# Eight operand turns on TensorE instead of by DMA, and a new order table, in a clustered-attention and MoE kernel

## The chip, the cores and the metric

The kernel runs on one core of a Trainium2 chip. The metric is the device time of one execution in microseconds (us). Beside it stand the span and the rows of one profiled execution. Five engines take part, each with its own queue of instructions: TensorE (PE in the rows; PEld is its loading of weights), VectorE (DVE), ScalarE (ACT), GpSimd (POOL) and SyncE (SP), which here issues all DMAs.

## The reference

```python
mask = q_assign[:, :, :, None] == k_assign[:, :, None, :]      # argmax over 16 centroids, per head
scores = np.where(mask, scale * np.matmul(q, k.transpose(0, 1, 3, 2)), -1000000000.0)
attn = softmax(scores)
x = (attn @ v).transpose(0, 2, 1, 3).reshape(3072, 512)
h = x @ w_in                                                   # 512 -> 2048
P = a[0] + a[1] * h + a[2] * h**2 + a[3] * h**3
Q = 1.0 + abs(b[0]) * abs(h) + abs(b[1]) * h**2
out = (P / (Q + 1e-06)) @ w_out                                # 2048 -> 512
```

(The softmax is abridged.) There are 4 batches, 8 heads, 768 tokens and 64 columns a head; a query attends only to keys of its own cluster.

## The kernel before, in words

All work is written down first as a list of operations (`Plan.op`), each with its engine, its tiles and the tiles it claims. `ORDER` then gives for every engine the sequence in which these operations are issued, as a list of their numbers; this table was found ahead of time by a search with a planner's durations, and while the kernel is built the table alone decides. SBUF tiles come from rings of buffers (`buf`), PSUM tiles from rings of banks (`bank`): tag "s" has two slots, for scores and products.

Heads are worked on in pairs, four pairs to a batch (so `sk_1` below is head pair 1 of the batch in hand). `prep` (from line 916 on) loads q and k of a pair, finds a power-of-two scale for each (squares on ScalarE, a maximum over the partitions by a transpose at line 964, a 1x1 maximum `m1` at 966 and a matmul at 968 that spreads it), and splits each into a high and a low f16 half, in tiles `tk` and `tq` of [128, 2, 6, 128], tokens on the partitions. There are four such tiles a pair: k1, q1, k2, q2. Each must be turned, so that the 128 columns lie on the partitions: `turn` (line 1059) does it with one DMA transpose of twelve 128x128 blocks, `sk` from `tk` and `sq` from `tq`. From the turned k1 and q1 come the logits against the centroids (`ptl`, line 1085), from those the one-hot cluster rows (line 1116) that are written into k2 and q2, and only then are k2 and q2 turned.

Batch 0 goes through `attend_keys`: scores `s` (1301), their row maxima `top` on VectorE (1310), the maxima written as correction rows into `tq` (to line 1344), a second turn of q2, the product `z` (1362) with keys on the partitions, its exponential on ScalarE, the context `px` (1381, 1387), and normalising (1409 to 1440, 1424 on TensorE). Batches 1 to 3 go through `attend` (scores at 1181, masked maximum at 1197, exponential, turn of the probabilities by DMA at 1241, context at 1254). `moe` has the first product `ph` (1511), the rational function on VectorE, ScalarE and GpSimd, and the second product `po` (1622). The weights of the MoE are loaded (`rwi`, `rwo`), scaled and converted (`wwi`, `wwo`, lines 669 to 757) while batch 0 is under way. `v_scale` loads v of a batch once ahead of its use (`rvm`, four loads a batch), squares it on ScalarE (line 526 is the helper that issues every ScalarE activation) and finds its scale (783 to 790). `centroid_norm` (566 to 602) prepares the centroids (`cslot`).

Of the kernel before, what the change touches and what calls it, by code (L numbers as in the profile page):

```python
# [10 lines left out]
F32 = mybir.dt.float32  # L11
F32R = mybir.dt.float32r
F16 = mybir.dt.float16
# [6 lines left out]
P = 128  # L20
# [7 lines left out]
K = {'ghd': 0.0, 'rvp': 0, 'look': 62.89, 'mulp': 0.4, 'sub': 0, 'xn': 14, 'NR': 8, 'sgp': 1, 'scp': 1, 'vsc': 0.75, 'sup0': 0, 'stk': 2, 'lop': 0, 'mgp': 0, 'rvn': 2, 'tq2': 2, 'at': 3, 'es': 4, 'vn': 3, 'ah': 5, 'rel': 0, 'twin': 1}  # L28
# [36 lines left out]
""",  # L65
    "DVE": """
# [313 lines left out]
def clustered_attention_moe_kernel(  # L380
# [89 lines left out]
    def token(name, cap):  # L470
        return Buf(None, name, cap, False)
# [1271 lines left out]
```

## Time and profile before

| what | value |
|---|---|
| three runs | 928.95, 930.76 (median), 934.13 us |
| the profiled execution | 927.86 us |
| its span | 926.1 us |
| busy in the span | PE 93%, DVE 87%, ACT 82%, POOL 65% |
| first row maximum of batch 0 (`top`) | 37.73 us from the span's start |
| first MoE product (`ph`) | 209.43 us |

A busy share is an average over the whole span. The two last lines mark borders within it: before 209.43 the program works on batch 0's attention and on the weights (called stage A), afterwards the MoE of one batch runs beside the attention of the next. In rows, x is the number of instructions that were put together, and a bracket tells how long the engine sat idle before and what ended that.

### The profile page before, as it was taken

Reading aid. Unit: us, or ns where it says so; the run is one execution under the profiler, and the core shown is the slowest. Engines: PE = TensorE matmul, PEld = TensorE weight load, DVE = VectorE, ACT = ScalarE, POOL = GpSimd, SP = SyncE. Lnnn points to the kernel's source line nnn. Section 1 sums busy time; section 2 is a strip of 40 time slices with the busy share of each in tenths; the row PEclk is TensorE's granted clock in tenths of the full one; section 3 lists DMA queues with packets and bytes.
Section 4 is the critical chain, followed back from the end, with each engine's and each line's share of the span. In section 5 each row is a group of like instructions: output and inputs, shape, how many; then the busy total and the mean of one; then the engine's idle time right before and its main releaser. Section 6 shows DMA issues by size and latency. Waiting matters only on the chain. (4 is left out here: it accounts for less than half of the span.)

```text
span 926.1 us, 20282 instructions
## 1 busy us (share of the span) xinstructions
PE 859.2 (93%) x7705; PEld 586.4 (63%) x7705; DVE 809.5 (87%) x1618; ACT 763.8 (82%) x1182; POOL 604.0 (65%) x627
## 2 busy tenths in 40 slices
PE   1559998997999999999999999999999999999997
PEld 1346675765676666667667676666666667766664
DVE  5789899658999999999999999999999998777776
ACT  5656675878998999998999999999998898766674
POOL 1347627398888776888888788868877766322221
PEclk9979999999999999999999999999999999999999
DMA  9996774666677797886869698898758667500000
GB/s 280 295 259 186 171 172 125 184 135 148 124 131 166 138 202 145 165 168 156 157 110 201 123 168 167 173 145 169 161 107 163 123 140 107 83 24 24 1 24 23
DMA packets 357345, 132.95 MB, mean 144 GB/s; under 512 B 335104, under 2 KB 351488, under 8 KB 357248
## 3 DMA queue, kind: packets, MB, share of 16 engines
q1 hardware_dynamic: 357248, 131.67, 67.5%
q8 instruction: 60, 0.98, 0.4%
q14 instruction: 37, 0.30, 0.1%
HBM read 41.98 MB, written 6.29 MB: 52 GB/s over the span
## 5 line engine op out<-in xcount | busy, mean ns | idle before, releaser
L1622 PE MATMUL po<-wout,u 128*128 128x512 f16 x1152 | 266.1, 379 | 1.4 <-ACT ob L526 0.8
L1511 PE MATMUL ph<-x,win 128*128 128x256 f16 x2304 | 266.1, 273 | 1.2 <-DVE x L1270 0.9
L1511 PEld LDWEIGHTS <-win 128*128 128x128 f16 x2304 | 225.1, 98 | 39.7 <-issue 3.2
L1551 POOL TENSOR_TENSOR s<-s,u 128x512 f32<-128x512 f32 x96 | 131.0, 1382 | 117.9 <-ACT s L526 85.7
L1622 PEld LDWEIGHTS <-u 128*128 128x128 f16 x1152 | 111.0, 98 | 122.2 <-issue 3.4
L1234 DVE SCALAR_TENSOR_TENSOR ah<-s,su,ah 128x768 f16<-128x768 f32 x144 | 143.3, 1012 | 8.9 <-ACT ah L526 7.5
L1197 DVE TENSOR_SCALAR_CACHE_REDUCE s<-s,cc 128x768 f32<-128x768 f32 x144 | 144.6, 1018 | 7.4 <-PE s L1181 6.8
L526 ACT ACTIVATE ah<-s,su 128x768 f16<-128x768 f32 x144 | 127.1, 904 | 15.3 <-ACT s L526 7.2
L526 ACT ACTIVATE s<-s,nm 128x768 f32<-128x768 f32 x144 | 126.5, 879 | 12.8 <-DVE s L1197 9.6
L1574 POOL TENSOR_TENSOR s<-s,u 128x512 f32<-128x512 f32 x72 | 103.5, 1448 | 28.7 <-ACT u L526 28.5
L1181 PE MATMUL s<-sk,sq 128*128 128x384 f16 x576 | 113.6, 328 | 8.5 <-DVE ah L1234 3.9
L1611 POOL TENSOR_TENSOR u<-s,u 128x512 f16<-128x512 f32 x72 | 86.5, 1213 | 30.6 <-ACT u L526 16.9
L1181 PEld LDWEIGHTS <-sq 128*128 128x128 f16 x576 | 52.7, 98 | 52.3 <-DVE ah L1234 13.0
L1254 PE MATMUL px<-at,vhi 128*64 128x256 f16 x864 | 74.8, 275 | 1.2 <-DVE df L1100 0.7
L526 ACT ACTIVATE u<-ph 128x512 f32<-128x512 f32 x96 | 57.5, 601 | 19.9 <-PE ph L1511 19.4
L1532 DVE TENSOR_TENSOR t<-ph,t 128x512 f32<-128x512 f32 x96 | 65.4, 682 | 9.0 <-ACT t L526 8.7
L1254 PE MATMUL px<-at,vlo 128*64 128x256 f16 x432 | 61.3, 273 | 0.0
L1604 DVE SCALAR_TENSOR_TENSOR s<-s,t 128x1024 f32<-128x1024 f32 (+1 forms) x49 | 58.7, 1197 | 1.7 <-POOL s L1574 0.7
L1254 PEld LDWEIGHTS <-vhi 128*64 128x64 f16 x864 | 47.9, 110 | 15.7 <-issue 8.2
L526 ACT ACTIVATE u<-t 128x1024 f16<-128x1024 f32 (+1 forms) x49 | 51.2, 1045 | 6.1 <-DVE t L1594 3.0
L526 ACT ACTIVATE t<-ph,gk 128x512 f32<-128x512 f32 x72 | 56.1, 784 | 0.0
L1537 DVE SCALAR_TENSOR_TENSOR t<-t,gk,ph 128x512 f32<-128x512 f32 x72 | 53.0, 740 | 0.9
(213 smaller groups left out, 1520.7 us busy)
## 6 DMA issues: line engine op xcount, KB each, us to landing
rwi<-in_moe_w_in_dram SPq DMA_DIRECT2D x16, 512.0 KB, 5.4
rwo<-in_moe_w_out_dram SPq DMA_DIRECT2D x16, 512.0 KB, 5.4
rk<-in_k_dram SPq DMA_DIRECT2D x32, 192.0 KB, 3.3
rq<-in_q_dram SPq DMA_DIRECT2D x32, 192.0 KB, 3.0
rvm<-in_v_dram SPq DMA_DIRECT2D x16, 384.0 KB, 5.6
rv<-in_v_dram SPq DMA_DIRECT2D x16, 384.0 KB, 4.0
out_dram<-ob SPq DMA_DIRECT2D x11, 512.0 KB, 3.2
at<-ah SPq DMA_TRANSPOSE x144, 3.9
```

What stands on the lines that cost most here:

```text
L526: lambda: nc.scalar.activation(out=out(), in_=in_(), func=func, **{a: (x() if callable(x) else x) for a, x in kw.items()}),
L1181: nc.tensor.matmul(sc.ap[:, i, :SH], lhsT=st["q" + x].ap[:, j, t, :], rhs=st["k" + x].ap[:, j, ks, :].rearrange("p t c -> p (t c)"), start ...
L1197: lambda nm=nm, view=view: ts(out=view(), in0=view(), scalar1=cc.ap, scalar2=None, op0=ALU.mult, op1=ALU.min, accum_out=nm.ap),
L1234: lambda part=part, view=view, su=su: stt(out=part(1), in0=view(), scalar=su.ap, in1=part(0), op0=ALU.mult, op1=ALU.subtract),
L1254: nc.tensor.matmul(px.ap[j * D : (j + 1) * D, :], lhsT=vv.ap[:, j, kt, :], rhs=at[j].ap[:, p_, kt].rearrange("p t c -> p (t c)"), start=(i ...
L1511: nc.tensor.matmul(ph[i].ap[:, fi * TW : (fi + 1) * TW], lhsT=win[f // 4][:, wpart, c, f % 4 * P : (f % 4 + 1) * P], rhs=xs[c].ap[:, xpart ...
L1532: lambda i=i, th=th, ph=ph: tt(out=th[i].ap, in0=ph[i].ap, in1=th[i].ap, op=ALU.mult),
L1551: lambda i=i, sh=sh, uh=uh: nc.gpsimd.tensor_tensor(out=sh[i].ap, in0=sh[i].ap, in1=uh[i].ap, op=ALU.mult),
L1574: lambda i=i, sh=sh, uh=uh: nc.gpsimd.tensor_tensor(out=sh[i].ap, in0=sh[i].ap, in1=uh[i].ap, op=ALU.mult),
L1604: lambda tw=tw, sw=sw: stt(out=sw(), in0=sw(), scalar=2.0, in1=tw(), op0=ALU.subtract, op1=ALU.mult),
L1611: lambda i=i, sh=sh, gl=gl, g16=g16, e=(nc.vector if gld else nc.gpsimd): e.tensor_tensor(out=gl[i].ap, in0=sh[i].ap, in1=g16()[:, 0, i * ...
L1622: nc.tensor.matmul(po[ti].ap, lhsT=g16()[:, part, c0 : c0 + P], rhs=wout[f // 4][:, wpart, f % 4], start=(k == 0 and f == f_first), stop=( ...
```

## The change

`turn` gets a second way. For head pairs 0 and 1 of batch 0 (`'pet': '_01'`) each of the four tiles is turned by twelve TensorE transposes into a PSUM bank of tag "s", and one copy of 1536 columns brings it to SBUF: on ScalarE for k, on VectorE for q. That is eight turns out of 68 of `sk` and `sq`; the second turn of q2, behind the correction rows, stays a DMA. The 1x1 maxima now lie in one of four zeroed [128, 1] columns, and the spreading matmul uses all 128 rows of `ones`. The `ORDER` table is replaced as a whole. `avs` and `xl` have values with which nothing differs.

```diff
@@ K
-... 'rel': 0, 'twin': 1}
+... 'rel': 0, 'twin': 1, 'pet': '_01', 'avs': 3}
@@ set-up
+    columns = [cp.tile([P, 1], F32, name=f"column{i}") for i in range(4)]
+    def column(name):
+        return Buf(lambda i: (name, columns[i])[1], "m1", len(columns), False)
...
+    ident16 = cp.tile([P, P], F16, name="ident16")
+    nc.gpsimd.tensor_copy(out=ident16, in_=ident)
...
+    for x in columns:
+        nc.vector.memset(x, 0.0)
@@ v_scale, and the same in prep
-        m1 = buf([1, 1], F32, "m1", f"vmm{b}", 4)
-        dve(195, lambda: nc.vector.tensor_reduce(out=m1.ap, in_=pt.ap[0:1, :], axis=AX.X, op=ALU.max), [pt], [m1], vt)
+        m1 = column(f"vmm{b}")
+        dve(195, lambda: nc.vector.tensor_reduce(out=m1.ap[0:1], in_=pt.ap[0:1, :], axis=AX.X, op=ALU.max), [pt], [m1], vt)
...
-            "PE", 310, lambda: nc.tensor.matmul(pb.ap, lhsT=ones[0:1, :], rhs=m1.ap, start=True, stop=True),
-            [m1], [pb], vt, mode=2,
+            "PE", 310, lambda: nc.tensor.matmul(pb.ap, lhsT=ones, rhs=m1.ap, start=True, stop=True),
+            [m1], [pb], vt,
@@ prep
-        def turn(x, u):
+        def turn(x, u, by_pe=False):
+            if by_pe:
+                tb_ = bank([P, 2 * NT, P], F16, "s", f"pt{x}{n}", 2)
+                def blocks(x=x, tb_=tb_):
+                    for i in range(2 * NT):
+                        nc.tensor.transpose(
+                            out=tb_.ap[:, i], in_=tm[x].ap.rearrange("p h t c -> p (h t) c")[:, i], identity=ident16
+                        )
...
+                op("PE", 1000, blocks, [tm[x]], [tb_], u, [st[x]])
+                if x[0] == "k":
+                    act(ac(2 * NT * P, 0, True), copied, source, AF.Copy, [tb_], [st[x]], u)
+                else:
+                    dve(dc(2 * NT * P), lambda: nc.vector.tensor_copy(out=copied(), in_=source()), [tb_], [st[x]], u)
+                return
...
+        by_pe = b == 0 and str(hp) in kn("pet", "")
         for x in ("k1", "q1"):
-            turn(x, vt + kc("p2", b, 2))
+            turn(x, vt + kc("p2", b, 2), by_pe)
...
         for x in ("k2", "q2"):
-            turn(x, vt + kc("p4", b, 4))
+            turn(x, vt + kc("p4", b, 4), by_pe)
```

What the new table does shows at three places. In its rows a name carries the pair (with `rvm`, `rwi` and `rwo` the piece) and a running number, and line numbers of the changed kernel are some 9 to 35 higher. The first place is SyncE's queue near its start. Before, behind the loads of the first k and q (`rk_0`, `rq_0`), it holds these loads and turns:

```order
L540 DMA rvm_2_123<-in_v_dram 128x2x384
L540 DMA cslot<-in_centroids_dram 128x64
L540 DMA rvm_1_127<-in_v_dram 128x2x384
L540 DMA rvm_0_129<-in_v_dram 128x2x384
L540 DMA rvm_0_131<-in_v_dram 128x2x384
L540 DMA rwi_2_136<-in_moe_w_in_dram 128x1024
L540 DMA rwi_1_138<-in_moe_w_in_dram 128x1024
L540 DMA rvm_3_145<-in_v_dram 128x2x384
L540 DMA rwi_0_171<-in_moe_w_in_dram 128x1024
L1059 DMA_TRANSPOSE sk_0_182<-tk_0_133 128x12x128
L540 DMA rk_1_189<-in_k_dram 128x384
L1059 DMA_TRANSPOSE sq_0_206<-tq_0_142 128x12x128
```

After the change it begins with:

```order
L549 DMA cslot<-in_centroids_dram 128x64
L549 DMA rk_0_129<-in_k_dram 128x384 x2
L549 DMA rq_0_132<-in_q_dram 128x384 x2
L549 DMA ab<-in_moe_b_dram 128x2
L549 DMA rwi_2_137<-in_moe_w_in_dram 128x1024
L549 DMA rvm_3_141<-in_v_dram 128x2x384
L549 DMA ab<-in_moe_a_dram 128x4
L549 DMA rwi_1_160<-in_moe_w_in_dram 128x1024
L549 DMA rvm_0_162<-in_v_dram 128x2x384
L549 DMA rwi_0_166<-in_moe_w_in_dram 128x1024
L549 DMA rk_1_217<-in_k_dram 128x384 x2
L549 DMA rvm_1_224<-in_v_dram 128x2x384
```

The centroids come first instead of behind five loads, a pair's turns are gone from it, and of the 16 `rvm` loads only the four of batch 0 stand here; those of batch 1 are issued shortly ahead of the first `ph`, the other eight behind it.

The second place is VectorE's queue just ahead of the first row maximum of pair 0. Before:

```order
L674 SCALAR_TENSOR_TENSOR wwo_0_335<-rwo_1_304,wwo_0_335 128x512
L618 TENSOR_SCALAR ev_408<-vp_ln 128x1
L621 RECIPROCAL ev_408<-ev_408 128x1
L787 TENSOR_REDUCE vmm_411<-vt_399 1x1
L681 SCALAR_TENSOR_TENSOR wwo_0_335<-rwo_1_304,wwo_0_335 128x512
L1036 SCALAR_TENSOR_TENSOR tq_1_318<-rq_1_235,qsc_1_373,tq_1_318 128x12x64
L618 TENSOR_SCALAR wie<-wip_ln 128x1
L621 RECIPROCAL wis<-wie 128x1
L1052 COPY tk_1_428<-tk_1_296 128x12x64
L1052 COPY tq_1_430<-tq_1_318 128x12x64
L1310 TENSOR_REDUCE top_0_439<-s_0_0_1_419 128x1
```

After the change (`ptq` is the PSUM bank with the turned q blocks):

```order
L1085 COPY sq_0_411<-ptq_0_393 128x1536
L678 TENSOR_SCALAR wwo_0_334<-wwo_0_334 128x512
L1019 RECIPROCAL qsc_1_385<-qsc_1_385 128x1
L683 SCALAR_TENSOR_TENSOR wwo_0_334<-rwo_1_337,wwo_0_334 128x512
L690 SCALAR_TENSOR_TENSOR wwo_0_334<-rwo_0_246,wwo_0_334 128x512
L1061 COPY tk_1_458<-tk_1_257 128x12x64
L1045 SCALAR_TENSOR_TENSOR tq_1_344<-rq_1_255,qsc_1_385,tq_1_344 128x12x64
L709 SCALAR_TENSOR_TENSOR wig_435,wia_465<-wig_435,ident 128x128
L690 SCALAR_TENSOR_TENSOR wwo_0_334<-rwo_1_337,wwo_0_334 128x512
L1061 COPY tq_1_484<-tq_1_344 128x12x64
L678 TENSOR_SCALAR wwo_1_463<-wwo_1_463 128x512
L1342 TENSOR_REDUCE top_0_492<-s_0_4_1_467 128x1
```

The second copy of pair 0 now stands in front of the maxima, among the same kind of weight conversions and the split of pair 1.

The third place is TensorE's queue around the first `ph`. Before, it ends stage A with the scores of batch 1 and the last normalising product of batch 0:

```order
L1181 LDWEIGHTS sq_0_2627
L1181 MATMUL s_0_0_1_2744<-sk_0_2617,sq_0_2627 128x384
L968 MATMUL kb_2_2752<-km_2_2736,ones 128x1
L1424 MATMUL px_3_2_2661<-rs_3_2_2727,pick 128x128 x2
L1511 LDWEIGHTS win_103
L1511 MATMUL ph_0_0_0_2770<-x_0_0_1321,win_103 128x256
```

After the change, `ph` follows a product z of pair 3, third block of queries:

```order
L1394 MATMUL z_3_2_1_0_2670<-sq_3_1502,sk_3_1212 128x256
L1394 LDWEIGHTS sk_3_1763
L1394 MATMUL z_3_2_1_0_2670<-sq_3_1830,sk_3_1763 128x256
L1546 LDWEIGHTS win_113
L1546 MATMUL ph_0_0_0_2683<-x_0_0_1150,win_113 128x256
```

And some forty rows behind it stand what came ahead of `ph` before:

```order
L1212 LDWEIGHTS sq_0_2557
L1212 MATMUL s_0_0_0_2725<-sk_0_2581,sq_0_2557 128x384
L1456 MATMUL px_3_1_2610<-rs_3_1_2677,pick 128x128 x2
L1212 LDWEIGHTS sq_0_2308
L1212 MATMUL s_0_0_1_2737<-sk_0_2221,sq_0_2308 128x384
```

So scores of batch 1 and the last context and normalising products of batch 0 have moved behind the first `ph`.

## Rows read from the trace of the kernel before

**Rows 1.** The page: busy times, and TensorE in forty slices of the span.

```profile
PE 859.2 (93%) x7705; PEld 586.4 (63%) x7705; DVE 809.5 (87%) x1618; ACT 763.8 (82%) x1182; POOL 604.0 (65%) x627
...
PE   1559998997999999999999999999999999999997
```

**Rows 2.** Busy times of the engines in four stretches; the first line names the columns.

```profile
core 0: us, PE busy (x) PEld busy (x) DVE busy (x) ACT busy (x) POOL busy (x), PEclk, DMA share, GB/s
0.00:36.10 36.10, 9.55 (x85) 6.96 (x85) 22.24 (x77) 21.53 (x45) 8.60 (x25) 1.00 0.99 297
36.10:74.80 38.70, 27.16 (x189) 17.20 (x189) 33.16 (x74) 21.75 (x40) 16.73 (x20) 0.82 1.02 274
74.80:157.20 82.40, 76.28 (x890) 53.05 (x890) 75.72 (x151) 53.65 (x92) 49.98 (x72) 1.00 0.64 158
...
240.00:800.00 560.00, 553.04 (x4803) 374.61 (x4801) 525.62 (x1066) 520.35 (x801) 440.71 (x407) 1.00 0.79 150
```

**Rows 3.** The same view for four other stretches: up to the first maximum, then the rest.

```profile
0.00:37.70 37.70, 11.15 (x90) 7.79 (x91) 23.80 (x81) 21.53 (x45) 8.60 (x25) 1.00 0.98 297
37.70:169.20 131.50, 113.25 (x1215) 78.03 (x1215) 117.35 (x241) 81.95 (x142) 68.19 (x92) 0.95 0.74 192
37.70:74.80 37.10, 25.55 (x184) 16.37 (x182) 31.59 (x69) 21.75 (x40) 16.73 (x20) 0.82 1.03 274
175.30:209.40 34.10, 31.59 (x455) 23.85 (x455) 16.83 (x53) 27.93 (x49) 29.21 (x48) 1.00 0.57 128
```

**Rows 4.** VectorE in order of time: start, duration, operation, idle time before and releaser.

```profile
8.57 0.23 DVE L566 TENSOR_TENSOR cslot<-cslot 128x64 f32<-128x64 f32 x1 [7.20 <-DMA cslot<-in_centroids_dram]
...
9.77 0.16 DVE L978 TENSOR_SCALAR qsc<-qb 128x1 int32<-128x1 int32 x1 [0.35 <-PE qb L968]
...
12.32 1.02 DVE L1036 SCALAR_TENSOR_TENSOR tk<-rk,ksc,tk 128x768 f16<-128x768 f32 x1 [0.58 <-DMA rwi<-in_moe_w_in_dram]
...
13.25 0.35 DVE L1052 COPY tk<-tk 128x768 f16<-128x768 f16 x1
...
169.00 0.19 DVE L1344 TENSOR_SCALAR tq<-rest 128x12 f16<-128x12 f32 x1
```

**Rows 5.** TensorE in order of time, from pair 3's z to the first `ph`.

```profile
175.30 1.36 PE L1362 MATMUL z<-sq,sk 128*128 128x256 f16 x11 [0.20 <-DMA sq<-tq]
...
200.24 2.81 PE L1381 MATMUL px<-at,rv 128*64 128x256 f32 x24
202.98 1.52 PE L1387 MATMUL px<-at,ones 128*32 128x128 f32 x48
...
209.43 1.47 PE L1511 MATMUL ph<-x,win 128*128 128x256 f16 x12
```

**Rows 6.** TensorE in order of time: a single transpose and two groups of sixteen products.

```profile
5.15 0.37 PE L964 MATMUL kt<-ident,sumk 128*1 128x128 f32 x1 [5.15 <-ACT tk L526]
...
30.33 1.89 PE L695 MATMUL wig<-wwi 128*128 128x128 bf16 x16
...
70.84 1.09 PE L695 MATMUL wig<-wwi 128*128 128x128 bf16 x16
```

**Rows 7.** Groups by line and form: busy us, mean ns of one | idle before, releaser.

```profile
L1310 DVE TENSOR_REDUCE top<-s 128x1 f32<-128x768 f32 x48 | 43.5, 947 | 1.2 <-PE s L1301 1.1
...
L526 ACT ACTIVATE at<-z,cc 128x768 f32<-128x768 f32 x48 | 41.8, 896 | 5.9 <-PE z L1362 5.9
...
L526 ACT ACTIVATE ob<-po,g 128x1024 f32<-128x1024 f32 x8 | 8.9, 1113 | 0.1
...
L526 ACT ACTIVATE rvm<-rvm 128x768 f32<-128x768 f32 x16 | 13.3, 834 | 8.1 <-DMA rvm<-in_v_dram 4.9 <-POOL tk L1116 3.2
```

**Rows 8.** DMA issues: the centroids, with their size and us from issue to landing.

```profile
cslot<-in_centroids_dram SPq DMA_DIRECT2D x1, 32.0 KB, 5.5
```

**Rows 9.** Line 1059, the turns by DMA, in the first 81 us.

```profile
DMA to landing us min/median/max: 4.2/5.0/7.9
```

**Rows 10.** ScalarE in order of time: one conversion that waited for its load.

```profile
40.15 0.67 ACT L526 ACTIVATE wwi<-rwi 128x512 f32<-128x512 f32 x1 [4.20 <-DMA rwi<-in_moe_w_in_dram]
```

More of the change, by code (lines that the diff above doesn't have):

```diff
@@ L25 @@
 M_BIG, M_MID, M_LOW = 2.0 ** 15, 2.0 ** 7, 2.0 ** -4
-K = {'ghd': 0.0, 'rvp': 0, 'look': 62.89, 'mulp': 0.4, 'sub': 0, 'xn': 14, 'NR': 8, 'sgp': 1, 'scp': 1, 'vsc': 0.75, 'sup0': 0, 'stk': 2, 'lop': 0, 'mgp': 0, 'rvn': 2, 'tq2': 2, 'at': 3, 'es': 4, 'vn': 3, 'ah': 5, 'rel': 0, 'twin': 1}
+K = {'ghd': 0.0, 'rvp': 0, 'look': 62.89, 'mulp': 0.4, 'sub': 0, 'xn': 14, 'NR': 8, 'sgp': 1, 'scp': 1, 'vsc': 0.75, 'sup0': 0, 'stk': 2, 'lop': 0, 'mgp': 0, 'rvn': 2, 'tq2': 2, 'at': 3, 'es': 4, 'vn': 3, 'ah': 5, 'rel': 0, 'twin': 1, 'pet': '_01', 'avs': 3}
 ORDER = {
     "ACT": """
[32 rows of a table removed]
[32 rows of a table added]
 """,
     "DVE": """
[45 rows of a table removed]
[45 rows of a table added]
 """,
     "PE": """
[26 rows of a table removed]
[26 rows of a table added]
 """,
     "POOL": """
[20 rows of a table removed]
[20 rows of a table added]
 """,
     "SP": """
[12 rows of a table removed]
[12 rows of a table added]
 """,
@@ L206 @@
     MORE = {("ACT", "POOL"): 95.0, ("DVE", "POOL"): 60.0, ("POOL", "ACT"): -30.0, ("ACT", "ACT"): 120.0, ("PE", "DVE"): 65.0, ("DVE", "ACT"): 50.0}
-    DMA = {"turn": (1440.0, 4100.0, 1700.0), "w": (430.0, 3900.0, 1350.0), "v": (450.0, 3900.0, 1100.0),
-           "qk": (430.0, 3000.0, 500.0), "few": (350.0, 2500.0, 200.0), "o2": (340.0, 3800.0, 1310.0), "o1": (340.0, 2300.0, 700.0)}
-    QUEUE = 950.0
+    DMA = {"turn": (1500.0, 4100.0, 1750.0), "w": (500.0, 4000.0, 1400.0), "v": (500.0, 4000.0, 1150.0),
+           "qk": (500.0, 3100.0, 520.0), "few": (350.0, 2500.0, 200.0), "o2": (340.0, 3800.0, 1310.0), "o1": (340.0, 2300.0, 700.0)}
+    QUEUE = 1300.0
     SWITCH = 105.0
@@ L455, in share @@
         return math.floor((i + 1) * f + 1e-6) > math.floor(i * f + 1e-6)
-    KEYMAJOR = {(0, int(hp)) for hp in kn("km", "0123")}
+    KEYMAJOR = {(0, int(hp)) for hp in kn("km", "0123") if hp != "_"}
     plan.look = kn("look", 40.0)
@@ L964, in over_partitions @@
             op("PE", 110, lambda: nc.tensor.transpose(out=pt.ap[0:1, :], in_=sums[nm].ap, identity=ident), [sums[nm]], [pt], u, chain="prep")
-            m1 = buf([1, 1], F32, "m1", f"{nm}m{n}", 4)
-            dve(195, lambda: nc.vector.tensor_reduce(out=m1.ap, in_=pt.ap[0:1, :], axis=AX.X, op=ALU.max), [pt], [m1], u)
+            m1 = column(f"{nm}m{n}")
+            dve(195, lambda: nc.vector.tensor_reduce(out=m1.ap[0:1], in_=pt.ap[0:1, :], axis=AX.X, op=ALU.max), [pt], [m1], u)
             pb = misc([P, 1], F32, f"{nm}b{n}")
-            op("PE", 310, lambda: nc.tensor.matmul(pb.ap, lhsT=ones[0:1, :], rhs=m1.ap, start=True, stop=True), [m1], [pb], u, mode=2)
+            op("PE", 310, lambda: nc.tensor.matmul(pb.ap, lhsT=ones, rhs=m1.ap, start=True, stop=True), [m1], [pb], u)
             return pb
@@ L1054, in prep, with copied, source @@
                 )
-        def turn(x, u):
+        def turn(x, u, by_pe=False):
[6 more added lines that the diff above has]
+                        )
+                def copied(x=x):
+                    return st[x].ap.rearrange("p h t c -> p (h t c)")
+                def source(tb_=tb_):
+                    return tb_.ap.rearrange("p i c -> p (i c)")
+                op("PE", 1000, blocks, [tm[x]], [tb_], u, [st[x]])
[4 more added lines that the diff above has]
+                return
             op(
@@ L1263, in attend @@
         x = buf([P, 2, TW], F16, "x", f"x{n}_{tb}", kn("xn", 14))
-        for k0 in range(0, NT, 3):
-            op("PE", 1000, lambda k0=k0: av(k0, k0 + 3), [vhi, vlo, *at], [px], u, [x], mode=1)
+        step = kn("avs", 3)
+        for k0 in range(0, NT, step):
+            op("PE", 1000 * step // 3, lambda k0=k0: av(k0, k0 + step), [vhi, vlo, *at], [px], u, [x], mode=1)
         xt[b, tb, hp] = x
@@ L1346, in attend_keys @@
         )
-        turn("q2", vts[0] + 1 + kc("kdt", b))
+        turn("q2", vts[0] + 1 + kc("kdt", b), str(hp) in kn("peq", ""))
         ev = bs[b]["ev"]
@@ L1437, in attend_keys @@
             act(300, lambda x=x: x.ap[:, 0], lambda rw=rw: rw.ap, AF.Copy, [rw], [x], ux, [rs])
+            xl = share("xl", hp * NB + tb)
             op(
-                "POOL", 630,
-                lambda x=x, rw=rw: nc.gpsimd.tensor_tensor(out=x.ap[:, 1], in0=rw.ap, in1=x.ap[:, 0], op=ALU.subtract),
-                [rw], [x], ux, [rs],
+                *(("DVE", 330) if xl else ("POOL", 630)),
+                lambda x=x, rw=rw, e=(nc.vector if xl else nc.gpsimd): e.tensor_tensor(
+                    out=x.ap[:, 1], in0=rw.ap, in1=x.ap[:, 0], op=ALU.subtract
+                ),
+                [rw], [x], ux, [rs], lock=True,
             )
```

270 rows, old and new, of the table ORDER are left out of this document.

## Prediction

> **What bounds the kernel now.** I read the page first, then the busy times by stretch, then each engine in order of time around the borders that matter. The page has TensorE busy 93% of the span, but its slices differ: the first two hold 1 and 5 tenths, nearly all from the seventh on 9 [rows 1]. By stretch [rows 2], TensorE is busy 9.55 us of the first 36.1, 27.16 of the next 38.7, 76.28 of the 82.4 after that, and from 240 to 800 98.8%. So there are two stages. Up to the first MoE product `ph` at 209.43 something feeds TensorE too slowly; behind it, time is TensorE work. What stage A saves moves that border to the left, and what is moved behind the border is paid there.
>
> In stage A the feeder is VectorE. It works 23.80 of the 37.7 us up to the first row maximum, and 117.35 of the 131.5 (89%) up to the end of the last correction of head pair 3 at 169.2 [rows 3, 4]. That correction still has to be turned by DMA: pair 3's product z goes on at 175.30, 6.1 us later [rows 5]. From there to `ph` pass 34.1 us, TensorE busy for 31.59 [rows 3]. DMA is the second suspect: it is busy all of the first 74.8 us (shares 0.99 and 1.02), and 0.64 behind them [rows 2].
>
> **The change, term by term.** All terms stand against the profiled execution: span 926.1, its own time 927.86, so 1.8 lie around the span. It is 0.3% under the median of the runs (930.76).
>
> *Added.* 96 transposes of one [128,128] block, and eight copies of 1536 columns. No row shows a 16-bit transpose. The nearest are groups of sixteen 128-column products, which took 1.89 us once and 1.09 once, 118 or 68 ns each [rows 6]: 0.8 to 1.4 us a turn, 6.5 to 11.3 in all. I cost them at nothing: they stand where TensorE idles 26.55 and 11.54 us [rows 2]; without that cover they would cost those 6.5 to 11.3.
> By the Trainium skill ("VectorE: DVE Perf Modes", section "The three transpose paths") a 128x128 transpose takes 390 ns on TensorE, by estimate 4.7 us a turn; that speaks against the change, and the rows' version of it is the last rival below.
> The copies: VectorE takes 0.35 us for a 768-column copy within SBUF [rows 4] and 0.947 for a maximum over 768 f32 columns from PSUM [rows 7]. So 1536 columns from PSUM cost 0.70 to 1.9; I take 1.75, near the upper row, because the source is PSUM. Four on VectorE: 7.0 (2.8 to 7.6). ScalarE takes 896 ns for 768 and 1113 for 1024 columns from PSUM [rows 7], so 1113 + 512 x 217/256 = 1547 ns. Four are 6.2 us, and ScalarE idles 14.6 and 16.95 in the first two stretches [rows 2]; that hides them, unless they queue behind a conversion that waits (a rival below).
> The zeroed columns cost VectorE four memsets while it waits for its first load, and the matmul against them is one instruction as before: nothing.
>
> *Work rearranged on VectorE.* By the order, ahead of pair 3's last correction stand the four copies (+7.0) and six small normalising rows that came later before (+1.6 by their durations in the trace), and no longer one scaling of `tq` (some 1.0 [rows 4]), a third of a weight conversion (1.8) and a few short maxima (1.0). Net +4.8.
>
> *Idle time removed.* Before the first maximum VectorE idles 37.7 - 23.8 = 13.9. The largest piece, 7.20, waits for the centroids, which land at 8.57 [rows 4], issued behind five other loads. They are now issued first, at about 0.7, and 5.5 us to landing [rows 8] make it 6.2: 2.4 saved. Their chain of short rows can then fill the four small waits between 9.77 and 12.32 (2.0 in all, first and last in [rows 4]). Turns of pair 0, which took 4.2 to 7.9 us to land [rows 9], become 0.8 to 1.4 plus the copy, and I let this end 1.5 of the remaining 4.7. Together 5.9: 8.0 are left.
> From the first maximum to the last correction it idles 131.5 - 117.35 = 14.15, of that 37.1 - 31.59 = 5.5 up to 74.8 [rows 3]. Most of these 5.5 follow ScalarE's conversions of weights, which wait for loads themselves, 4.20 us at 40.15 [rows 10]. Eight turns, and the twelve loads of `v` for batches 1 to 3, no longer share the DMA with those loads. I let 3.1 go: 11.0 are left. What is late next is the correction's turn, still by DMA, at 6.1.
>
> *The sum.* Last correction of pair 3: 141.15 + 4.8 + 8.0 + 11.0 = 165.0 (before 169.2). Plus 6.1: 171.1 for z of pair 3 (175.3). From z to `ph` the order takes out 10.9 of TensorE's 31.6 us: 9.4 go behind `ph` (the last context product, 2.81 + 1.52 [rows 5], and eight scores, four picks, six z products and short rows with about 5.1), 1.5 ahead of z; 34.1 x 20.7/31.6 = 22.3. First `ph` at 193.4. Behind it stay 926.1 - 209.4 = 716.7, plus the 9.4: span 919.5, time **921**, which is 0.7% under its own 927.86 and 1.0% under the median. In short: 4.2 us from VectorE's supply, 2.4 because the idle share between z and `ph` shrinks with its rows and 1.5 of them run earlier, and 9.4 carried over the border for nothing.
>
> *Bounds.* Copies at 0.70: 4.2 less, 917. All of the 5.5 gone too: 914.5. Half of the 6.1 too, with fewer entries on SP's queue: 911.5. Idle after the first maximum unchanged: 924. The forecast's own range is 911 to 926.
>
> **Rivals.**
> *No saving arrives (same).* The copies only take the place of waiting, and the idle times stay at 13.9 + 14.15. Then the last correction is at 141.15 + 4.8 + 28.05 = 174.0, `ph` at 202.4, the time 921 + 9 = **930**. For it: 7 us more on the engine that feeds, and weights still come by the full DMA. Against: the idle rows end with loads. A variant: eight squares of `v` (834 ns each, 6.7 us [rows 7]) leave stage A for a stage in which ScalarE is busy 520 of 560 us [rows 2]; should all of it land on TensorE's path, 928. Chances 0.16 and 0.07.
> *PSUM slots (slower).* The turned blocks sit in the two-slot ring "s" that the scores use. A slot is held until its copy has run, and copies run in their engine's order: those of k on ScalarE, behind conversions that can wait 4.20 for a load [rows 10]. Such a wait stops the next scores, and with them VectorE's maxima. Two of them on top of the case without savings give 930 + 8.4, **938**. It decides (0.5% above the median, 935.4) from 5.4 us of stalls when nothing is saved, or 14 against the forecast's savings. Against: up to 74.8 TensorE idles 38 us and ScalarE 31 [rows 2], so a stall can hide. Chance 0.11.
> *Dear transposes (slower).* One f32 transpose alone takes 370 ns [rows 6]. At that price a turn is 4.4 us plus its copy, about 3.4 more than counted; the four of pair 0 stand in front of the first scores, 13.6, and half of pair 1's 13.6 would show too: 921 + 20 = **941**. It decides from 14 us more. Against: sixteen products in a row come to 68 ns each. Chance 0.06.
>
> **Numbers.** The forecast has 0.60, the same cases 0.23, the slower ones 0.17; 0.5% either way is about what a measurement of this kernel can tell from no change. The range reaches from the forecast's lower end into the cases above: 910 to 936.
>
> **What would show it.** Right: the centroids' first row near 6.2; a turn's twelve transposes in 0.8 to 1.4 us; VectorE's copies near 1.75; the first maximum still at about 37, but with two copies done; last correction of pair 3 near 165, z 6 later, `ph` near 193, and 726 us of span behind it. Wrong, if the transposes wait for slots and the wait is named after a maximum or a copy; if VectorE's idle time up to the last correction is still near 28; or if the part behind `ph` grows by more than 10.

## The result, and the profile after

The changed kernel takes 916.75 us (median of 915.67 to 920.27) against 930.43 for the kernel before in the same comparison (928.95 to 934.13): a ratio of 0.9854, 95% interval 0.9814 to 0.9893, so 1.5% faster. Run again later, it gave 0.9867 (0.9830 to 0.9903). The forecast was 921, or 0.7% to 1.0% faster, with a range of 910 to 936: the way and the range were right, the gain is larger than forecast.

The page of the changed kernel, with the two lines that answer to [rows 1]:

```profile
span 913.8 us, 20484 instructions
...
PE 858.2 (94%) x7801; PEld 591.4 (65%) x7801; DVE 810.5 (89%) x1626; ACT 768.5 (84%) x1186; POOL 593.8 (65%) x628
...
PE   3689999897999999889999999999999999999997
```
TensorE is busy as long as before (858.2 against 859.2 us, the 96 transposes included) in a span that is 12.3 shorter. The first three slices read 3, 6 and 8 where they read 1, 5 and 5: the gain is near the start. The stretches that answer to [rows 2, 3] are cut here at the changed kernel's own borders: first maximum, last correction of pair 3, pair 3's z, first `ph`; the last line is the first 74.8 us as a whole.

```profile
0.00:35.50 35.50, 14.79 (x150) 11.54 (x151) 26.05 (x86) 22.11 (x38) 8.34 (x28) 1.00 0.71 243
35.50:162.10 126.60, 116.29 (x1331) 82.43 (x1330) 116.38 (x236) 79.97 (x134) 70.09 (x89) 0.96 0.56 150
166.30:188.20 21.90, 20.25 (x290) 15.81 (x290) 14.45 (x42) 21.27 (x43) 16.30 (x29) 1.00 0.88 250
0.00:74.80 74.80, 47.58 (x461) 32.88 (x465) 64.18 (x158) 41.05 (x66) 28.93 (x53) 0.95 0.60 189
```
VectorE now idles 35.5 - 26.05 = 9.45 us before the first maximum (13.9 before) and 126.6 - 116.38 = 10.22 from there to the last correction (14.15). DMA's share in the first 74.8 us is 0.60, where it was 0.99 and 1.02. VectorE in order of time at the marks of [rows 4]:

```profile
2.63 0.22 DVE L575 TENSOR_TENSOR cslot<-cslot 128x64 f32<-128x64 f32 x1 [1.23 <-DMA cslot<-in_centroids_dram]
...
12.26 1.00 DVE L1045 SCALAR_TENSOR_TENSOR tk<-rk,ksc,tk 128x768 f16<-128x768 f32 x1
...
35.54 2.68 DVE L1342 TENSOR_REDUCE top<-s 128x1 f32<-128x768 f32 x3
```
```profile
161.42 0.65 DVE L1376 TENSOR_SCALAR tq<-rest 128x12 f16<-128x12 f32 x1
```
The last correction ends at 162.07 (169.2 before). TensorE, first with the new turns and the first scores, then at the marks of [rows 5]:

```profile
13.32 1.46 PE L1071 MATMUL ptk<-ident,tk 128*128 128x128 f16 x12 [3.67 <-DVE tk L1045]
...
26.65 1.44 PE L1071 MATMUL ptk<-ident,tk 128*128 128x128 f16 x12
...
34.10 1.95 PE L1333 MATMUL s<-sk,sq 128*128 128x384 f16 x11 [2.22 <-ACT sk L535]
...
36.54 0.83 PE L1071 MATMUL ptq<-ident,tq 128*128 128x128 f16 x12 [0.38 <-DVE top L1342]
```
```profile
166.33 0.71 PE L1394 MATMUL z<-sq,sk 128*128 128x256 f16 x5 [1.62 <-DMA sq<-tq]
...
188.19 2.78 PE L1546 MATMUL ph<-x,win 128*128 128x256 f16 x24
190.81 0.81 PE L1212 MATMUL s<-sk,sq 128*128 128x384 f16 x4
191.46 0.61 PE L1456 MATMUL px<-rs,pick 128*128 128x128 f32 x4
```
Twelve transposes take 1.46 us early on and 0.83 later, that is 122 and 69 ns each, as the two groups of [rows 6] had it. Pair 3's z goes on at 166.33 and `ph` starts at 188.19, 21.2 us earlier than before. Right behind `ph` stand the scores of batch 1 and a normalising product. Behind `ph` the span has 913.8 - 188.2 = 725.6 us, 8.9 more than the 716.7 before. So 21.2 were gained ahead of the border and 8.9 of them paid behind it: 12.3. These borders are read from one execution each. The profile of the repeat (experiment 8) has the last correction at 161.0, z at 165.3, `ph` at 189.0 and 727.1 us behind it, so single borders hold to some 1.5 us.

The turned blocks by tile (minimum, median and maximum in ns), first VectorE's for q, then ScalarE's for k:

```profile
L1071 PE MATMUL ptq<-ident,tq x48: 216/254/314, 15.3 to 54.6; 128*128 128x128 f16 x48
L1085 DVE COPY sq<-ptq x4: 944/948/958, 17.4 to 55.5; 128x1536 f16<-128x1536 f16 x4
```
```profile
L535 ACT ACTIVATE sk<-ptk x4: 1431/1444/1451, 15.3 to 55.6; 128x1536 f16<-128x1536 f16 x4
```
And the centroids' load, as in [rows 8]:

```profile
cslot<-in_centroids_dram SPq DMA_DIRECT2D x1, 32.0 KB, 1.9
```

### The profile page after: what moved, and what is told of

It reads as the page before. It is cut to its first block, busy times and chain, and to the rows that moved or that the text cites. A ratio compares the mean times of both kernels' runs of the same rounds, so it can differ in the third digit from the quotient of the medians.

```text
span 913.8 us, 20484 instructions
## 1 busy us (share of the span) xinstructions
PE 858.2 (94%) x7801; PEld 591.4 (65%) x7801; DVE 810.5 (89%) x1626; ACT 768.5 (84%) x1186; POOL 593.8 (65%) x628
## 5 line engine op out<-in xcount | busy, mean ns | idle before, releaser
L1586 POOL TENSOR_TENSOR s<-s,u 128x512 f32<-128x512 f32 x96 | 123.9, 1307 | 103.1 <-ACT s L535 87.6
L1609 POOL TENSOR_TENSOR s<-s,u 128x512 f32<-128x512 f32 x72 | 104.0, 1458 | 27.7 <-ACT u L535 27.5
L1646 POOL TENSOR_TENSOR u<-s,u 128x512 f16<-128x512 f32 x72 | 83.8, 1174 | 51.6 <-DVE s L1639 23.9
L1567 DVE TENSOR_TENSOR t<-ph,t 128x512 f32<-128x512 f32 x96 | 65.5, 684 | 13.0 <-ACT t L535 12.2
L1639 DVE SCALAR_TENSOR_TENSOR s<-s,t 128x1024 f32<-128x1024 f32 (+1 forms) x49 | 61.7, 1259 | 0.5
L535 ACT ACTIVATE u<-t 128x1024 f16<-128x1024 f32 (+1 forms) x49 | 51.1, 1042 | 10.4 <-DVE t L1629 5.6
L1285 PEld LDWEIGHTS <-vhi 128*64 128x64 f16 x864 | 46.0, 110 | 17.1 <-issue 7.2
```

What stands on the lines that cost most here:

```text
L535: lambda: nc.scalar.activation(out=out(), in_=in_(), func=func, **{a: (x() if callable(x) else x) for a, x in kw.items()}),
L1285: nc.tensor.matmul(px.ap[j * D : (j + 1) * D, :], lhsT=vv.ap[:, j, kt, :], rhs=at[j].ap[:, p_, kt].rearrange("p t c -> p (t c)"), start=(i ...
L1567: lambda i=i, th=th, ph=ph: tt(out=th[i].ap, in0=ph[i].ap, in1=th[i].ap, op=ALU.mult),
L1586: lambda i=i, sh=sh, uh=uh: nc.gpsimd.tensor_tensor(out=sh[i].ap, in0=sh[i].ap, in1=uh[i].ap, op=ALU.mult),
L1609: lambda i=i, sh=sh, uh=uh: nc.gpsimd.tensor_tensor(out=sh[i].ap, in0=sh[i].ap, in1=uh[i].ap, op=ALU.mult),
L1639: lambda tw=tw, sw=sw: stt(out=sw(), in0=sw(), scalar=2.0, in1=tw(), op0=ALU.subtract, op1=ALU.mult),
```

## The experiments

Two theories were on the table. Theory A: turning on TensorE shortens the way to the scores and frees DMA, and this by itself makes the gain. Theory B: the new order makes it, and the turns trade waiting for copies. Every ratio below is to the kernel before on the same chip, with its 95% interval. Experiments 1 to 3, 4 to 7, 8 to 11 and 12 ran on four different chips, so a comparison across these sets goes by the ratios.

### 1. The turns without the new order

```diff
 (changed kernel)
-ORDER = the new table
+ORDER = the table of before; per turn one SP entry out, one PE entry in at its place in time,
+        one ACT (k) or DVE (q) entry some 1.5 us later
```

> The order of before, with the eight turns of pairs 0 and 1 on TensorE: twelve transposes at the place in TensorE's queue at which SyncE issued the turn, the copy in its engine's queue about 1.5 us of rows later. Theory A (the shorter turns and the DMA time they free make most of the gain): 919 to 925, DMA share up to 74.8 well under 1.0 and the last correction of pair 3 before 166. Theory B (the new order makes most of it, and the turns by themselves only trade waiting for copies): 927 to 934, with the 3.8 us of copies on VectorE showing as later maxima.

Measured: 934.43 us, ratio 1.0044 (1.0023 to 1.0065), slower. Theory A falls in this form. The stretches up to the first maximum and on to the last correction, and the first 74.8 us:

```profile
0.00:39.30 39.30, 15.92 (x153) 12.61 (x154) 25.51 (x87) 26.20 (x49) 8.10 (x26) 0.79 0.74 255
39.30:171.60 132.30, 116.54 (x1246) 81.60 (x1245) 117.72 (x243) 82.55 (x143) 70.40 (x92) 0.91 0.64 175
0.00:74.80 74.80, 43.77 (x367) 32.21 (x368) 58.16 (x156) 48.45 (x89) 25.18 (x46) 0.75 0.79 251
```
DMA is relieved (0.79 instead of 1.0), and still VectorE idles 13.8 + 14.6 = 28.4 us, as before (28.05), and its rows, the copies among them, are 2.1 us longer (143.2 against 141.15): the last correction ends at 171.6. That border alone proves no loss (experiment 3 has it at 172.3 with the time of before); that the front gains nothing shows in VectorE's and TensorE's rows:

```profile
33.81 0.96 DVE L1085 COPY sq<-ptq 128x1536 f16<-128x1536 f16 x1 [0.41 <-PE ptq L1071]
```
```profile
35.69 0.38 PE L717 MATMUL win<-wia,ones 128*128 128x1 f32 x2 [1.25 <-DVE qsc L1019]
...
37.26 0.56 PE L799 MATMUL vb<-column,ones 128*128 128x1 f32 x2 [1.06 <-DVE column L796]
37.68 1.44 PE L1333 MATMUL s<-sk,sq 128*128 128x384 f16 x4
```
The last turned tile of pair 0 is in SBUF at 34.8, but in the old order its scores stand in TensorE's queue behind small products for a weight's and v's scale, two of which wait 1.25 and 1.06 us for VectorE. So the scores start at 37.68 and the first maximum at 39.34 (37.73 before). VectorE is later itself: at 31.27 it waits 1.45 us for a small product that now stands behind a turn (0.34 before, at 30.43). In the changed kernel pair 0's scores start at 31.55 and go on at 34.10. In the first 74.8 us TensorE's granted clock, which has the levels 1.2 and 2.4 GHz, averages 0.75 of the higher one here, 0.91 in the kernel before and 0.95 in the changed kernel; whether that cost anything, and what makes up the 0.4%, was not taken apart.

### 2. The new order without the turns

```diff
-K = {... 'pet': '_01', ...}
+K = {... 'pet': '_', ...}
 ORDER (new table): eight SP entries put where TensorE's transposes stood in time; those and the copies out
```

> The new order with the eight turns back on DMA, each issued where TensorE's transposes stood in time; nothing else changed. Theory A: 925 to 935, since four times 0.95 us leave VectorE but each turn lands 4 to 8 us after its issue and pair 0's maxima start late (near 40 instead of 35.5). Theory B: 914 to 920, VectorE has less to do and the loads of v are out of the way anyway.

Measured: 928.75, ratio 0.9991 (0.9965 to 1.0016): the same as before. Theory B falls too. TensorE and VectorE in order of time:

```profile
38.87 3.68 PE L1333 MATMUL s<-sk,sq 128*128 128x384 f16 x11 [5.13 <-DMA sk<-tk]
...
63.75 4.36 PE L1333 MATMUL s<-sk,sq 128*128 128x384 f16 x15 [5.14 <-DMA sk<-tk]
```
```profile
38.85 0.36 DVE L1061 COPY tk<-tk 128x768 f16<-128x768 f16 x1 [4.27 <-DMA sk<-tk]
...
41.57 2.85 DVE L1342 TENSOR_REDUCE top<-s 128x1 f32<-128x768 f32 x3
```
The first maximum comes at 41.57 (35.54 with the turns on TensorE; theory A had said near 40); TensorE waits 5.13 us for pair 0's turned k and 5.14 for pair 1's, VectorE 4.27 because a tile may not be overwritten before its turn has read it. `ph` starts at 196.3, 13.2 earlier than before, but 727.3 - 716.7 = 10.6 of that is work carried behind it. So neither part gains alone, and together they gain 1.5%. That is a third theory, C: an order saves VectorE's waiting only if what it puts forward is ready, and the shorter turns make it ready. The rows show both sides of it: in experiment 1 pair 0's operands are ready at 34.8 and the order asks for them at 37.68, here TensorE asks from 33.7 on and they come at 38.87. Neither experiment had an order made for it: the turns were put into a table that had not been searched with them.

### 3. Centroids first, alone

```diff
 (kernel before)
-ORDER["SP"] = "... 3 at its sixth place ..."
+ORDER["SP"] = "3 first, the rest as it was"
```

> The kernel before with one entry moved: the centroids' load is the first on SyncE's queue. Prediction's term (2.4 us of waiting saved at the front and handed on to the first product of the MoE): 928. Rival: the scales of k and q, which wait for their own loads, set the front, so the wait only changes its name: 930 to 931, first maximum still at 37.5 to 38.

Measured: 929.87, ratio 0.9997 (0.9979 to 1.0014).

```profile
0.00:37.90 37.90, 11.20 (x91) 7.74 (x92) 23.89 (x82) 21.54 (x45) 8.53 (x25) 1.00 0.98 293
37.90:172.30 134.40, 113.48 (x1211) 77.91 (x1211) 116.94 (x241) 81.92 (x142) 69.87 (x92) 0.94 0.74 188
```
VectorE still idles 14.0 us before the first maximum, at 37.9. The wait only changes its name, as the rival had it. In the changed kernel too the first scaling of `tk` starts at 12.26, where it was 12.32 [rows 4].

### 4 to 6. Tripled copies and transposes

```diff
 (changed kernel, one edit each)
+4: VectorE's copy of ptq three times
+5: ScalarE's copy of ptk three times
+6: each block transposed three times: for i in 3 * list(range(2 * NT))
```

> The changed kernel with each of VectorE's four copies done three times: eight more rows of 0.95 us, 7.6 in all, ahead of pair 3's last correction. If VectorE sets the pace of the stage (the prediction), nearly all of it arrives: last correction at 168 to 170 instead of 162.1, time 922 to 925. If its 19.7 us of idle time there swallow them: 917 to 919.

> The changed kernel with each of ScalarE's four copies done three times: eight more rows of 1.44 us, 11.5 in all. If ScalarE's idle time covers its copies (the prediction): 917 to 920, last correction by at most 3 us later. Rival: k's copies stand in the chain in front of the scores, so that the length of each counts: 924 to 929.

> The changed kernel with each of the 96 transposes done three times: 192 more, about 18 us of TensorE by the 0.83 to 1.46 us a turn takes now. If TensorE's idle time covers the transposes (the prediction costs them at nothing): 917 to 922. Rival of dear transposes: 2.9 us more a turn, pair 0's four in a chain ahead of the first scores and half of pair 1's: 928 to 936.

Measured: 926.16, ratio 0.9964 (0.9944 to 0.9985); 929.63, ratio 1.0000 (0.9983 to 1.0018); 924.93, ratio 0.9949 (0.9928 to 0.9969). Against the changed kernel's 0.9867 these are 9.0 us for 7.6 of VectorE's copies, 12.4 for 11.5 of ScalarE's, and 7.6 for some 18 of transposes (twice the 9.3 of the changed kernel's eight turns); by the two intervals each of the three is uncertain by some 4 us either way. VectorE's bill was expected. ScalarE's was not: what was added to its copies arrives whole, although in the changed kernel it is busy only 41 of the first 74.8 us. The transposes lie in neither of the two expected ranges. VectorE's last correction, with its own copies tripled and with ScalarE's, and the first 74.8 us of the latter run:

```profile
167.89 0.65 DVE L1376 TENSOR_SCALAR tq<-rest 128x12 f16<-128x12 f32 x1
```
```profile
174.44 0.65 DVE L1380 TENSOR_SCALAR tq<-rest 128x12 f16<-128x12 f32 x1
```
```profile
0.00:74.80 74.80, 42.81 (x371) 28.87 (x372) 53.51 (x135) 45.20 (x63) 22.93 (x46) 0.93 0.55 164
```
With VectorE's copies tripled the correction ends at 168.5, as expected (168 to 170). With ScalarE's it ends at 175.1, 13.0 us later, where the prediction's reading had allowed 3; VectorE has nothing added, but gets 53.51 us of work done in the first 74.8, where it did 64.18. TensorE in the same run:

```profile
20.53 0.37 PE L973 MATMUL kt<-ident,sumk 128*1 128x128 f32 x1 [4.06 <-ACT tk L535]
...
33.31 1.44 PE L1071 MATMUL ptk<-ident,tk 128*128 128x128 f16 x12 [2.73 <-ACT sk L1085]
...
39.66 3.68 PE L1337 MATMUL s<-sk,sq 128*128 128x384 f16 x11 [2.88 <-ACT sk L1085]
...
67.13 4.96 PE L1337 MATMUL s<-sk,sq 128*128 128x384 f16 x15 [3.22 <-ACT sk L1085]
```
Pair 0's and pair 1's scores wait for the copy of k (2.88 and 3.22 us), a transpose waits for the slot that a copy still holds (2.73), and pair 1's scale waits (4.06) because its square stands behind the copy in ScalarE's queue. Idle time elsewhere on that engine does not help. With the transposes tripled, 7.6 of some 18 us arrive, between a fifth and two thirds by the intervals.

### 7. One more turn on TensorE

```diff
-K = {... 'pet': '_01', 'avs': 3}
+K = {... 'pet': '_01', 'peq': '_3', 'avs': 3}
 ORDER: pair 3's second q turn out of SP; in PE at its place in time, its copy in DVE 1.3 us later
```

> The changed kernel with one more turn moved: pair 3's second turn of q2, behind the correction rows, on TensorE with a copy on VectorE. By the sum's term (4.3 us from the last correction's end to z) the wait becomes 0.8 + 0.95 and some latency, z about 2 us earlier; TensorE had other rows in that time and idled only 1.6: 915 to 916.5. Rival: transposes and copy cost what they save, or their slot delays a score: 916.5 to 919.

Measured: 923.11, ratio 0.9927 (0.9900 to 0.9954), so 0.6% slower than the changed kernel, and slower than either expectation.

```profile
164.07 0.84 PE L1070 MATMUL ptq<-ident,tq 128*128 128x128 f16 x12
164.75 0.27 PE L1393 MATMUL z<-sq,sk 128*128 128x256 f16 x1
165.96 0.71 PE L1393 MATMUL z<-sq,sk 128*128 128x256 f16 x5 [0.94 <-DVE sq L1084]
```
```profile
180.70 0.85 ACT L534 ACTIVATE rvm<-rvm 128x768 f32<-128x768 f32 x1 [2.03 <-POOL tq L1146]
```
The last correction ends at 161.74, but the transposes stand behind a context product and start at 164.07; z goes on at 165.96, 4.2 us behind the correction, where it was 4.3 with the DMA. VectorE then waits for them (1.08 us) and copies while it has conversions to do, and what follows is late: ScalarE waits 2.03 for GpSimd at 180.70, in front of three of the four squares of batch 1's v, which the changed kernel has done by 180.6. `ph` starts at 192.65 instead of 188.19.

### 8 to 10. The mark, and one pair at a time

```diff
 8: the changed kernel itself
-K = {... 'pet': '_01', ...}
+9: 'pet': '_0', pair 1's turns in SP      10: 'pet': '_1', pair 0's turns in SP
 ORDER (new table): the entries moved as in experiment 2, for one pair
```

> The changed kernel itself once more, as the mark for the other three and for the runs with tripled work: 914 to 919 us.

> The new order, pair 0's four turns on TensorE and pair 1's back on DMA. In the run with all eight on DMA, TensorE waited 5.13 us for pair 0's turned k and 5.14 for pair 1's. If the two waits add: half of the way back, 921 to 924. If only the turns ahead of the first scores count: 917 to 919.

> The new order, pair 1's four turns on TensorE and pair 0's back on DMA. If the two waits add: 921 to 924, with the first maximum late as with all eight on DMA (about 41) and the 5 us wait in front of pair 1's scores gone. If only pair 0's turns count: 926 to 929.

Measured: 918.06, ratio 0.9867 (0.9830 to 0.9903); 919.49, ratio 0.9871 (0.9821 to 0.9921); 923.36, ratio 0.9931 (0.9904 to 0.9958). Pair 0's turns alone reach the changed kernel within the interval (919.49, just above the 917 to 919 expected if only they count). Pair 1's alone bring 0.6% against none, and 923.36 lies in the range for waits that add, although the first maximum stays late (42.29) and pair 0's wait (5.28) stays. So whether the waits add is not settled: the two gains, 1.2% and 0.6% against experiment 2, sum to 0.6 points more than the 1.2% of all eight turns, with an uncertainty of some 0.7 points. What is shown is that pair 0's turns bring most of the gain. In the profile of the run with pair 0 on TensorE the wait for pair 1's turned k is still there:

```profile
59.79 4.96 PE L1333 MATMUL s<-sk,sq 128*128 128x384 f16 x15 [5.03 <-DMA sk<-tk]
```
Whether that wait costs something once pair 0 is on TensorE stays open: this profiled execution (span 921.9) lies at the upper end of its own runs (915.52 to 923.82), and the intervals of 8 and 9 overlap almost whole. TensorE's granted clock does not sort the runs: in the first 74.8 us of the profiled executions it averages 0.95 and 0.98 for the changed kernel (spans 913.8 and 916.1), 0.98 in experiment 10 (921.3) and 0.93 in experiment 2 (923.6).

### 11. All copies on VectorE

```diff
-                if x[0] == "k":
+                if False:
 ORDER: four copies out of ACT, into DVE at the same place in time
```

> The changed kernel with ScalarE's four copies of k moved to VectorE, at the same place in time: 5.8 us less on ScalarE, 3.8 more on VectorE. By the rates of the runs with tripled copies (13 us of time for 11.5 of ScalarE's copies, about 9.4 for 7.6 of VectorE's) -6.5 + 4.7: 914 to 916. If VectorE is the one feeder and ScalarE's length only counted because it was tripled: 919 to 922.

Measured: 920.44, ratio 0.9900 (0.9858 to 0.9942). The value lies where the rival had it, above the estimate by rates (914 to 916), though the interval touches that. No run is under 918.69, and none of experiment 8, on the same chip, over 918.67: the faster copy (0.95 against 1.44 us) brings no gain on VectorE. So the rates of the tripled copies, uncertain by some 4 us each, do not carry over to taking the first copies away.

### 12. A third pair

```diff
-K = {... 'pet': '_01', ...}
+K = {... 'pet': '_012', ...}
 ORDER: pair 2's first four turns out of SP, into PE at their places in time, copies 1.5 us later
```

> The changed kernel with pair 2's four turns on TensorE as well, two more copies on VectorE (1.9 us) and two on ScalarE (2.9). In the trace of the changed kernel nothing between 35 and 160 us waits for a turn by DMA. So nothing is saved and the copies are paid: at about the rates of the tripled copies 2.3 + 3.2 us, 921 to 925. Rival: less DMA lets weights land earlier (ScalarE waits 4.9 us for them between 35 and 160): 914 to 918.

Measured: 922.72, ratio 0.9933 (0.9910 to 0.9955), 0.7% slower than the changed kernel. The chain of waits from 35 to 165 us (us in total, times, longest), and the stretch that ends at 162.1:

```profile
ACT sk L534 <- PE ptk L1070: 9.8, 3, 4.6
...
DVE top L1341 <- PE s L1332: 4.3, 3, 2.7
```
```profile
35.50:162.10 126.60, 113.92 (x1344) 81.18 (x1343) 111.03 (x225) 78.13 (x128) 66.79 (x85) 0.97 0.48 136
```
DMA's share falls to 0.48 (0.56), and nothing comes of it. ScalarE now stands 9.8 us in front of copies whose transposes have not run, its other rows behind it, VectorE waits 4.3 for scores (1.1 in the changed kernel), and it gets 111.0 us of work done in a stretch in which it did 116.4.

## Why the prediction was right, point by point

The sum's steps against the profiled executions (the changed kernel's own time is 915.67, 12.2 under the 927.86 that the sum was made against, where the forecast had 6.9):

| step | predicted | measured |
|---|---|---|
| rows of VectorE up to the last correction | 141.15 + 4.8 = 145.95 | 26.05 + 116.38 = 142.43 |
| its idle time, before and after the first maximum | 8.0 + 11.0 | 9.45 + 10.22 |
| end of the last correction of pair 3 | 165.0 | 162.1 |
| from there to z | 6.1 | 4.3 |
| from z to `ph` | 22.3 | 21.9 |
| behind `ph` | 716.7 + 9.4 | 725.6 |
| span | 919.5 | 913.8 |

**The feeder.** Right in part. VectorE's row work and idle time give the border within 0.4 us once its copies are taken at their real price, and 7.6 us more on it cost 9.0. But work added to ScalarE's copies costs as much (experiment 5): VectorE's idle time is itself set by the chain of copies in front of the scores, and VectorE is not the only feeder.

**A copy at 1.75.** Mis-sized, the largest miss: 0.95, between the bounds but nearer the lower one. Four make 3.2 of the 3.5 us by which VectorE's rows were overestimated. The choice followed the upper row because the source is PSUM; the f16 copy runs at 0.62 ns a column, where the maximum over f32 takes 1.23. The Trainium skill ("VectorE: DVE Perf Modes", section "The perf-mode tier table (the rule you actually need)") lets copies from PSUM run at up to twice the base rate; by the clock of 0.96 GHz that it gives (section "Specifications") this makes 0.8 us for 1536 columns, an estimate. The measured 0.95, 1.7 times the base rate, agrees, and that rule would have been the better choice.

**Turn and transposes.** The 69 and 122 ns are the rows' 68 and 118. The 390 ns of the Trainium skill ("VectorE: DVE Perf Modes", section "The three transpose paths") do not hold for transposes in a row, and the rival of dear transposes falls with them: a block takes 216 to 314 ns from start to end, but twelve in a row take 0.83 to 1.46 us. That they cost nothing is not shown: tripled, some 0.4 of each added microsecond arrives (0.2 to 0.6 by the intervals).

**ScalarE's copies hidden by its idle time.** Wrong: in the changed kernel itself the first scores wait 2.22 us for such a copy (at 34.10), and experiment 5 charges what is added to them whole. How much of the first 5.8 us was paid is not shown; experiment 11 takes them off ScalarE, for 3.8 us on VectorE, and gains nothing. The sum came out well because the idle time saved was estimated for VectorE as a whole, with these waits in it; that is luck.

**Idle time, by its reasons.** The total is right (19.0 against 19.7), two of the reasons are not, so here too there is luck in the sum. The centroids came far earlier than forecast (their first row at 2.63, not 6.2), and the 2.4 for them is nothing by itself (experiment 3); a late load in the new order was not tried. Relief of DMA saved nothing by itself either (experiments 1 and 12 have it and are slower). What saves is the front of pair 0, in an order that has work ready: experiments 2, 9 and 10.

**The wait from correction to z.** 4.3 instead of 6.1 with a turn still by DMA; the forecast had left it as it was. The repeat has 4.3 as well, and the new order with all turns by DMA 3.8 (experiment 2), so it goes with the order; why was not taken apart.

**Work carried over `ph`.** Right: 8.9 against 9.4, and 10.4 in the repeat, just past the 10 that was to be a sign of being wrong.

**The rivals.** "No saving arrives" came true in experiment 1, the turns without their order: idle 28.4, last correction 171.6. In the changed kernel it did not. Nor did its variant, the squares of v on TensorE's path: it would have put 6.7 us behind `ph` on top of the 9.4, and the part behind `ph` grew by 8.9 and 10.4. Of PSUM slots there is a trace only (a transpose waits 0.38 us for a maximum at 36.54; the 2.22 of the first scores is for the copy's result); with the copies tripled the slot shows (2.73).

What stays open: which part of the new order makes the difference between experiment 1 and the changed kernel. It moves loads, conversions, pair 1's scores and the normalising at once, and these were not tried one at a time. Nor has any run an order searched anew with the turns by DMA; that such an order could gain by itself is not excluded.

## What to carry to other kernels

In these runs a transfer replaced by an engine's work paid where a row of the trace waited for it: pair 0's turns did, a third pair's did not. The replacement stands in a queue with other work, so its price is not its duration beside the engine's idle share, but what waits for it and what stands behind it; the order has to be made for it, and neither half of such a change can be judged alone.

## What the runs showed of the hardware that was not expected

A 1536-column f16 copy from PSUM took VectorE 0.95 us and ScalarE 1.44. The centroids' load of 32 KB, which took 5.5 us to land as the sixth entry of SyncE's queue (4.3 in experiment 1), took 1.9 as the first (1.7 to 1.9 in experiments 2, 3 and 8).
